# 128 zero products, 192 columns wide, in eight places of TensorE's order in chunks 1 to 3

## The chip, the core and the metric

The kernel runs on one core of one Trainium2 chip. A core has a matrix engine (TensorE, PE in the profile; its weight loads are a row of their own, PEld), three engines for element-wise work (VectorE = DVE, ScalarE = ACT, GpSimd = POOL) and a queue that mostly issues transfers (SyncE = SP). Each engine works through its own list of instructions in order; where one needs another's result it waits on a semaphore. The metric is the device time of one execution in microseconds (us). Before the change it is 824.97 us, the median of five runs: 825.07, 822.38, 826.83, 820.85 and 824.97.

## The reference

Two blocks, one after the other. The first is a recurrence over 768 steps for each of 4 batches and 8 heads, with a 40 x 40 state:

```python
for t in range(S):
    kt, vt, rt = (k[:, :, t], v[:, :, t], r[:, :, t])
    wt, at, bt = (w[:, :, t], a[:, :, t], b[:, :, t])
    y[:, :, t] = np.einsum('bhd,bhde->bhe', rt, state)
    Sa = np.einsum('bhde,bhe->bhd', state, at)
    state_decay = state * wt[:, :, None, :] - np.einsum('bhd,bhe->bhde', Sa, bt)
    state = state_decay + np.einsum('bhd,bhe->bhde', vt, kt)
```

Its result, turned to 3072 tokens of 320 values, goes through the second block, whose weights are 320 x 2048 and 2048 x 320:

```python
h = x @ w_in
g = h * np.cos(h)
return (g @ w_out).astype(np.float32)
```

## The kernel before

The sequence is cut into 24 chunks of 32 steps (`NCH`). A chunk of the recurrence has five steps in a row, `t, q, x, s, z` (functions `ch_t` to `ch_z`): the state is transposed (`sT`, line 558), multiplied with r (`qps`), combined with products prepared for the chunk (`x0ps`), multiplied with the chunk's inverted triangle (`sps`, which needs `rt`), and added up to the new state and the output (`dps`). Preparation of coming chunks is cut into steps too: `v, k, g` turn v, r and k and form the products `gram` for the next chunk; `pw, pa, pb, pn` turn w, a and b (`wT`, `aps`, `bT`) and form `nps` for later pairs of chunks. For four chunks at a time the triangles are inverted on VectorE alone (`inv_step`, lines 468 and 472), ending in `rt` (line 476).

The second block is cut into pieces over groups of 256 tokens (two chunks) and four slices of the 2048 hidden values: `first_a` and `first_b` make `ph` = x @ w_in in two tiles, ACT and DVE turn these into `gT` = h cos h (lines 730 to 740), and `second` multiplies them with w_out and adds up in `po`, one tile for each chunk of the group, over the four slices. A piece can only run when its chunks' outputs are there.

The weights come as words of a wider type and are rounded on the chip (`rounded`): DVE and ACT take them apart, DVE multiplies, POOL puts the sign on. These steps run until about 150 us.

The order on every engine is written out by hand in one Python loop over the chunks: for each chunk there is a list `segs` of steps, in which `M` marks a place where one piece of the second block goes (`piece`). `step` runs one entry and then lets queued-up work follow: steps of the inversion and of the weights (`fill` says how many of each) and work put off with `later` (transfers above all, which SP issues in that order). Since every engine works in order, an entry that waits on TensorE holds up all products behind it.

In chunks 0, 1 and the beginning of 2 there are already products of zeros on TensorE that nobody reads: `busy(n)` issues n of them, 512 columns wide, in bfloat16, from the tile `idle`, after each step. `shifted` puts 111 and 75 products of one column in two places. `mm` (line 101) issues all products but the transposes, so they all have that line in the profile.

On-chip accumulators (PSUM) are three pools of two tiles each: `ps_a` for the recurrence, `ps_h` for `ph` and the existing zero products, `ps_o` for `po` and, early on, `aps`. A `po` tile has 512 columns, of which the sums take 320 (`DM`).

## Time and profile before

| | us |
|---|---|
| median of five runs | 824.97 |
| lowest, highest | 820.85, 826.83 |
| the profiled execution | 825.07 |
| its span, first to last instruction | 823.1 |
| TensorE busy | 745.8 (91%) |
| VectorE busy | 508.1 (62%) |
| ScalarE busy | 384.0 (47%) |
| GpSimd busy | 200.7 (24%) |
| mean granted clock of TensorE | 0.95 of full |

The page gives busy time by engine over the span, and rows of 40 digits, one for each fortieth (20.6 us), in tenths; the row of the granted clock says how fast TensorE was allowed to run. The timeline lists instructions in order of time: start, busy time, engine, line, operation, output and inputs, shape and count, and in brackets how long the engine had been idle before and what ended that ("issue": nothing that the profile shows). Ends of products are modelled, so groups can overlap by a few tenths of a microsecond. A table of stretches gives for each the busy time of every engine, with the count of instructions, and the granted clock. The chain of waits follows the work back from the last instruction to what released it, step by step.

### The profile page before, as it was taken

How to read it: one execution, taken by the hardware profiler on the slowest of the kernel's cores; microseconds unless marked ns; L12 is line 12 of the kernel's file. 1: busy time of each engine (PE TensorE's matmuls, PEld its weight loads, DVE VectorE, ACT ScalarE, POOL GpSimd, SP SyncE). 2: the span in 40 equal slices, each digit the busy share in tenths (PEclk: the TensorE clock that was granted, in tenths of full speed). 3: DMA queues.
4: the chain of work that ended last, by engine and by line, in shares of the span. 5: the costliest groups of instructions: out<-in, count | busy, mean ns of one | idle time of the engine just before them, and what ended most of it. 6: DMA issues, size and time to landing. Idle time of an engine off the chain costs nothing.

```text
span 823.1 us, 37673 instructions
## 1 busy us (share of the span) xinstructions
PE 745.8 (91%) x16832; PEld 571.0 (69%) x16832; DVE 508.1 (62%) x1081; ACT 384.0 (47%) x707; POOL 200.7 (24%) x352
## 2 busy tenths in 40 slices
PE   3657678899689999999999999999999999999997
PEld 2534456677457777777777777777787777777775
DVE  6987888859645599354797553895444874332231
ACT  1214677544244553545446446435635445363352
POOL 5215554430214023212221230330230222201000
PEclk9856899899789999999999999999999999999999
DMA  7356663244043322333224324214210212101000
GB/s 124 76 131 164 175 165 103 47 120 71 22 100 85 62 58 52 70 99 68 52 39 74 65 61 69 60 37 69 61 41 24 46 35 52 21 21 37 20 17 16
DMA packets 183297, 55.66 MB, mean 68 GB/s; under 512 B 157152, under 2 KB 178656, under 8 KB 183136
## 3 DMA queue, kind: packets, MB, share of 16 engines
q1 hardware_dynamic: 180560, 51.95, 28.8%
q8 instruction: 132, 2.16, 1.1%
q10 hardware_dynamic: 2320, 0.98, 0.5%
q0 software_dynamic: 256, 0.33, 0.2%
q14 instruction: 29, 0.24, 0.1%
HBM read 42.07 MB, written 11.14 MB: 65 GB/s over the span
## 4 chain that ended last, share of the span: by engine, by line
PE 61%; DVE 20%; ACT 6%; DMA 5%; issue 3%; SPq 3%; POOL 1%; DVEq 0%; ACTq 0%; POOLq 0%
PE ph L101 21%; PE po L101 19%; DVE inv_tmp L468 4%; DVE inv L472 4%; PE dps L101 3%; PE x0ps L101 3%; SPq L152 3%; DVE rw L391 3%; PE gram L101 2%; PE vT L326 2%; PE sps L101 2%; PE qps L101 1%; DVE turns L732 1%; PE nps L101 1%; PE sT L558 1%
## 5 line engine op out<-in xcount | busy, mean ns | idle before, releaser
L101 PE MATMUL po<-w_out_sb,gT 128*128 128x320 f32 x768 | 227.0, 445 | 0.0
L101 PE MATMUL ph<-xT,w_in_sb 128*128 128x256 f32 x768 | 189.4, 392 | 4.4 <-DVE gT L740 3.7
L101 PEld LDWEIGHTS po<-w_out_sb,gT 128*128 128x128 f32 x768 | 142.5, 193 | 55.9 <-issue 4.2
L101 PEld LDWEIGHTS ph<-xT,w_in_sb 128*128 128x128 f32 x768 | 142.5, 194 | 33.5 <-issue 13.8
L730 ACT ACTIVATE turns<-ph,rnd 128x512 f32<-128x512 f32 x96 | 63.9, 686 | 157.2 <-PE ph L101 156.7
L732 DVE SCALAR_TENSOR_TENSOR turns<-turns,ph 128x512 f32<-128x512 f32 x96 | 63.7, 683 | 108.9 <-ACT turns L730 108.5
L740 DVE TENSOR_TENSOR gT<-ph,turns 128x512 f32<-128x512 f32 x96 | 65.6, 685 | 36.3 <-ACT turns L737 36.3
L657 POOL TENSOR_TENSOR qz<-qz,wc 128x160 f32<-128x160 f32 x92 | 43.4, 490 | 159.3 <-DVE qz L656 158.7
L472 DVE TENSOR_TENSOR inv<-inv,inv_tmp 128x31 f32<-128x31 f32 (+15 forms) x186 | 71.9, 386 | 6.4
L468 DVE TENSOR_TENSOR inv_tmp<-u,inv 128x31 f32<-128x31 f32 (+15 forms) x186 | 70.2, 377 | 4.4
L736 ACT ACTIVATE turns<-turns 128x512 f32<-128x512 f32 x96 | 60.2, 627 | 23.5 <-DVE turns L732 23.5
L737 ACT ACTIVATE turns<-turns,half_pi 128x512 f32<-128x512 f32 x96 | 69.3, 722 | 3.1
L490 POOL COPY vp<-nat_v 128x320 f32<-128x320 f32 x25 | 12.2, 488 | 183.2 <-DMA nat_v<-in_v_dram 166.6
L101 PE MATMUL ph<-xT,w_in_tail 64*128 64x256 f32 x384 | 54.6, 403 | 0.0
L656 DVE TENSOR_TENSOR qz<-dps,qz 128x160 f32<-128x160 f32 x92 | 28.9, 314 | 34.6 <-PE dps L101 34.5
L391 DVE RECIPROCAL rw<-nat_w 128x320 f32<-128x320 f32 x20 | 42.8, 2141 | 0.1
L562 ACT COPY s<-sT 128x512 f32<-128x512 f32 x46 | 24.5, 584 | 38.0 <-PE sT L558 38.0
L101 PEld LDWEIGHTS ph<-xT,w_in_tail 64*128 64x128 f32 x384 | 33.2, 187 | 10.3 <-issue 6.6
L668 POOL TENSOR_TENSOR yt<-yt,wb 128x512 f32<-128x512 f32 x24 | 31.4, 1309 | 22.4 <-DVE yt L663 22.4
L546 ACT COPY vvm<-gram 128x256 f32<-128x256 f32 x24 | 8.8, 368 | 54.8 <-DVE ag L541 54.4
L101 PE MATMUL sps<-x,rt 32*32 32x72 f32 x1536 | 22.7, 239 | 11.3 <-DVE rt L476 9.0
L101 PEld LDWEIGHTS sps<-x,rt 32*32 32x32 f32 x1536 | 18.0, 109 | 21.4 <-issue 16.6
(118 smaller groups left out, 1067.9 us busy)
## 6 DMA issues: line engine op xcount, KB each, us to landing
words<-in_moe_w_in_dram SPq DMA_DIRECT2D x8, 512.0 KB
nat_k<-in_k_dram SPq DMA_DIRECT2D x96, 40.0 KB
nat_v<-in_v_dram SPq DMA_DIRECT2D x96, 40.0 KB
nat_r<-in_r_dram SPq DMA_DIRECT2D x96, 40.0 KB
xd<-yt SPq DMA_DIRECT2D x48, 80.0 KB
out_dram<-ot SPq DMA_DIRECT2D x24, 160.0 KB
nat_b<-in_b_dram SPq DMA_DIRECT2D x88, 40.0 KB
wd<-ws SPq DMA_DIRECT2D x5, 640.0 KB
```

The costliest lines, as they stand in the source:

```text
L101: nc.tensor.matmul(o, lhsT=lhsT, rhs=rhs, start=start, stop=stop, skip_group_check=True)
L391: nc.vector.reciprocal(rw, wn)
L468: nc.vector.tensor_tensor(tmp, u[:, j : j + 1, :j].to_broadcast([P, C - j, j]), x[:, j:, j : j + 1].to_broadcast([P, C - j, j]), ALU.mult,)
L472: nc.vector.tensor_tensor(x[:, j:, :j], x[:, j:, :j], tmp, ALU.subtract)
L656: nc.vector.tensor_tensor(z, pick(dp, 0, (2 * N72 + C, 2), (N72, 2), (1, D)), z, ALU.add)
L657: nc.gpsimd.tensor_tensor(z, z, wc.rearrange("p (f m b) -> p f m b", f=2, m=2)[:, :, :, bb] .unsqueeze(3).to_broadcast([P, 2, 2, D]), ALU. ...
L668: nc.gpsimd.tensor_tensor(yt.rearrange("p j b t -> p (j b) t"), yt.rearrange("p j b t -> p (j b) t"), wx, ALU.mult)
L730: nc.scalar.activation(n, u, ACTF.Identity, bias=rnd, scale=1.0)
L732: nc.vector.scalar_tensor_tensor(n, n, -ROUND, u, ALU.add, ALU.subtract)
L736: nc.scalar.activation(n, n, ACTF.Abs)
L737: nc.scalar.activation(n, n, ACTF.Sin, bias=half_pi, scale=-2.0 * math.pi)
L740: nc.vector.tensor_tensor(gT[:, 2 * e : 2 * e + 2].rearrange("p f t -> p (f t)"), us[e], ns[e], ALU.mult)
```

## The change

`second` keeps the whole tile of 512 columns and slices it where it is used. A new helper `kept_busy(n)` issues n products of the zero tile `idle`, 128 x 128 weights by 192 columns in bfloat16, into the columns 320 to 511 of a `po` tile: of the tile of the running sum where there is one (then it adds zeros there), otherwise of a fresh tile of the same pool. A table `FILL` says where: key (chunk, place in `segs`), value the number of products, issued ahead of that entry. In chunk 1 that is ahead of `x` (12) and `z` (16); in chunk 2 ahead of `t` (10), `q` (14), `k` (6) and of the third `M`, which is `first_a` of the second piece (37); in chunk 3 ahead of `q` (13) and of `pa4`, the transposes `aps` of chunks 4 and 5 (20). Together 128. The existing `busy` calls stay.

```diff
     def second(g, j, i):
 
         if j == 0:
-            G["po", i] = ps_o.tile([P, 512], F32, tag="o", name="po")[:, :DM]
-        po = G["po", i]
+            G["po", i] = ps_o.tile([P, 512], F32, tag="o", name="po")
+        po = G["po", i][:, :DM]
...
+        def kept_busy(n):
+
+            if not n:
+                return
+            ps = G.get(("po", 0))
+            if fresh := ps is None:
+                ps = ps_o.tile([P, 512], F32, tag="o", name="spare")
+            for m in range(n):
+                mm(ps[:, DM:], idle, pick(idle, 0, (0, 2), (1, (512 - DM) // 2)), fresh and m == 0)
...
+        FILL = {(1, 4): 12, (1, 7): 16, (2, 0): 10, (2, 2): 14, (2, 3): 6, (2, 8): 37, (3, 3): 13, (3, 4): 20}
         for c in range(NCH):
...
             for i, seg in enumerate(segs):
+                kept_busy(FILL.get((c, i), 0))
                 while seg is s and ("rt", c) not in G:
```

## The prediction

> **What bounds the kernel now.** I read the page first, then TensorE's timeline, then busy time in stretches of 3.41 us.

> ```profile
> PE 745.8 (91%) x16832; PEld 571.0 (69%) x16832; DVE 508.1 (62%) x1081; ACT 384.0 (47%) x707; POOL 200.7 (24%) x352
> PEclk9856899899789999999999999999999999999999
> PE 61%; DVE 20%; ACT 6%; DMA 5%; issue 3%; SPq 3%; POOL 1%; DVEq 0%; ACTq 0%; POOLq 0%
> ```

> TensorE is busy for 91% of the span and makes 61% of the chain that ended last. One digit of the clock row is 20.6 us: after about 245 us it is full to the end, before that it dips. So the kernel is bound by TensorE from about 245 us on, and what the change can move is when that long stage begins. The eight places lie between 84 and 146 us. TensorE's timeline shows the wait in each (start, busy time, and in brackets the idle time before with what ended it):

> ```profile
> 85.60 0.88 PE L101 MATMUL x0ps<-vvm,ag 32*32 32x72 f32 x64 [1.61 <-ACT qz L574]
> 99.42 0.32 PE L101 MATMUL dps<-idle 32*64 32x288 bf16 x4 [2.50 <-DVE sm L622]
> 103.19 1.38 PE L558 MATMUL sT<-ident,qz 128*128 128x128 f32 x8
> 108.47 0.86 PE L101 MATMUL qps<-rT,s 40*40 40x32 f32 x64 [1.52 <-ACT s L562]
> 111.38 0.63 PE L326 MATMUL kT<-ident,kn 128*128 128x128 f32 x4 [0.87 <-issue]
> 124.17 3.35 PE L101 MATMUL ph<-xT,w_in_sb 128*128 128x256 f32 x8 [3.75 <-DVE gT L740]
> 127.45 0.88 PE L101 MATMUL sps<-x,rt 32*32 32x72 f32 x64
> 142.37 0.81 PE L101 MATMUL qps<-rT,s 40*40 40x32 f32 x64 [1.46 <-ACT s L562]
> 145.26 1.97 PE L326 MATMUL aps<-ident,nat_a 128*128 128x128 f32 x8 [2.08 <-ACT wb L374]
> 163.90 0.63 PE L326 MATMUL aps<-ident,nat_a 128*128 128x128 f32 x4 [2.21 <-DMA nat_a<-in_a_dram]
> 213.13 1.25 PE L101 MATMUL sps<-x,rt 32*32 32x72 f32 x64 [7.53 <-DVE rt L476]
> ```

> Seven of the eight places are real waits for another engine; the one at 103.19 is not. The granted clock changes only at steps of 3.41 us, so I cut the trace there (stretch, length, TensorE busy, weight loads, DVE, ACT, POOL, then granted clock and DMA):

> ```profile
> 65.57:68.98 3.41, 3.41 (x139) 2.33 (x137) 1.48 (x5) 3.08 (x5) 0.11 (x1) 0.50 0.39 59
> 120.18:123.59 3.41, 0.25 (x28) 0.13 (x16) 2.74 (x7) 3.35 (x7) 1.44 (x2) 1.00 0.88 282
> 123.59:127.01 3.42, 2.83 (x7) 2.33 (x8) 2.92 (x6) 2.46 (x4) 0.93 (x3) 0.50 0.38 108
> 140.66:144.07 3.41, 1.06 (x66) 0.70 (x64) 3.41 (x5) 3.41 (x7) 2.11 (x2) 1.00 0.73 216
> 161.14:164.55 3.41, 1.20 (x9) 0.99 (x10) 1.91 (x1) 0.65 (x2) 0.86 (x1) 1.00 0.38 62
> 212.34:215.75 3.41, 2.62 (x67) 2.06 (x68) 1.44 (x4) 0.49 (x2) 0.00 (x0) 0.50 0.00 0
> 215.75:219.17 3.42, 3.42 (x22) 1.74 (x29) 1.76 (x1) 0.00 (x0) 0.86 (x1) 0.50 0.00 0
> ```

> A stretch with little work (0.25, 1.06, 1.20 us) is followed by one at half clock; one at half clock is left after a full stretch (3.41, 3.42, and also 2.83), not after 2.62. (A stretch with 2.17 us, mostly small products, at 89.46 also fell to half.) Zeros count: the full stretch at 65.57 was partly the existing zero products.

> **The change part by part.** *The edit of `second`* slices the same tile in another place; TensorE issues the same products. Nothing.

> *Removed, moved:* nothing. Instruction order shows 128 weight loads and 128 products more on TensorE, none of them waiting, and no wait changed on any engine. Only what is behind them on TensorE can be delayed.

> *Price of one.* Zero products 512 columns wide took 1.03 us for four and 1.25 for five at full clock, so 0.22 us each, 0.43 ns per column, 0.082 us for 192 columns. Upper end: eight 128-column f32 transposes with a weight load each took 1.04 us and four 0.60, so 0.11 each. I take 0.085, nearer the row with the same data and the same load; 128 of them are 10.9 us (10.5 to 14.1).

> *Place by place, work against wait, in us:* 12 are 1.02 against 1.61; 16 are 1.36 against 2.50; 10 are 0.85 with no wait; 14 are 1.19 against 1.52; 6 are 0.51 against 0.87; 37 are 3.15 against 3.75; 13 are 1.11 against 1.46; 20 are 1.70 against 2.08. So 10.0 of 10.9 us lie in waits. The uncovered 0.85 delays the transposes sT, which end at 104.57 and are copied by ACT only at 107.36, so 2.8 us of slack hides them; without it they would cost 0.85. At 0.11 the 37 overrun by 0.32, the 20 by 0.12 and the 14 by 0.02.

> *Instruction supply.* The instruction queue shows 132 packets and 2.16 MB for 33,664 loads and products, so about 256 instructions a packet. TensorE's waits marked "issue" inside gram (0.92, at 88.4) and sps (1.28, at 91.8) sit 256 instructions apart, so a block that comes late costs up to 1.3 us. The 256 added instructions make one block more and leave the later cuts where they were; between the places the cuts move. Ahead of the 37 one cut falls in the last products of gram (ends 120.4). Bounds: 0, or 1.3 less the 0.6 spare, so 0.7. I take 0.3, the middle, because no row decides it. [...]

> *What the zeros buy.* The 37 lift the stretch at 120.18 from 0.25 to about 3.2 us busy, so the next is granted full clock. The eight ph there took 3.35; the same eight took 1.99 at 117.21. That is 1.36, less 0.3: 1.06. It is on the path: sps follows at once, ACT's copy of it ends 2.38 us of idle time on DVE (sm at 128.89), ACT itself having idled 1.16 before it, so up to 1.16 passes. I take 1.0. From there the chain of waits runs over ph, ACT's turns and DVE's queue to the reciprocal at 150.66, the loads that SP issues behind it, and the nat_a that lands at 163.90: about 1.0 early all the way.
> The 13 and 20 lift the stretch at 140.66 from 1.06 to about 3, so the ones at 144.07 and 147.49 run at full clock: 5.6 us of half-clock work, up to 2.8. I count none, because DVE's queue (aT, reciprocal, 147 to 153 without a gap but 0.85) sets what comes next; if that cover is thin it is up to 2.8 more. The first five places buy nothing I count: ACT and DVE, busy with the weight words, release what follows.

> *Given on.* At 163.90 ph runs at half clock from 164.55. Starting 1.0 earlier, 1.0 more of it lies ahead of 164.55 at full clock, which saves 0.5: 1.5. DVE's inverse carries that to rt, so sps starts at 211.6, not 213.13. The stretch from 212.34 is then full and the half clock ends at 215.75, not 219.17. Of 6.04 us at half clock (3.02 at full) 4.1 are left, doing 2.05; the other 0.97 runs at full clock to 216.7: 2.45. The half-clock stretches from 236.23 I leave as they are. Sum: 825.07 (the profiled execution: span 823.1 and 2.0 around it) less 2.5, so 822.6; the median 824.97 lies 0.1 below it: **822.5 us.**

> [...]

> **The rivals.**
> *A, as above* (0.40): 821 to 824.
> *B, the clock gain grows* (0.33): with the chain early, the stretch at 161.14 holds about 1.65 us of work (rows at full clock stayed there with 1.81 and 1.89, fell with 1.20), and the one at 232.82 may also hold enough. The first turns the rest of the half-clock ph, 1.2, into gain; the second 5.97 us of half-clock work, 3.0; a thin cover at 144 up to 2.8. So 2.5 plus 1.2 to 5.8: 816.5 to 821.4, likely 819. For it: after 92 us TensorE does 30 us of work at half clock, so 15 are lost. Against: nothing fills the 2.2, 7.5 and 2.4 us waits behind the last place.
> *C, hidden* (0.10): the 1.0 us is eaten in DVE's queue, where weight conversion is back to back from 131 to 147, or the steps fall so that no half clock followed the 3.75 us wait: 824 to 826.
> *D, the 37 overrun* (0.17), the other side. They start when gram's last products have their block. From a start later than 121.0 (124.17 less 3.15) ph is late; at 121.7 by 0.7. If by then the stretch holds only some 2.1 us, it may still fall to half clock: the 15 left at 123.59 take 2.6, ph starts at 126.2 and ends 2 us later than now. Then the later steps fall worse by one stretch (1.7) or two: 826 to 831.

> **How the numbers follow.** A measurement of this kernel can tell about 0.5% from no change: below 820.85 is faster, above 829.1 slower. Faster: 0.30 of B and 0.07 of A, 0.37. Slower: 0.13 of D. Same: the rest, 0.50. Range: a tenth below is B with most of its terms, 816.5; a tenth above is D at its worse end, 829.5. A's own range is 821 to 824.

> **What would show it.** Right: eight groups of 192-column products at 0.082 to 0.09 us pitch, idle of 0.3 to 1.1 us left behind them, clock 1.00 where 123.59 to 127.01 and 144 to 151 are now 0.50, sps of chunk 2 about 1 us earlier, rt's waiter near 211.6, no step down in the clock after about 245. Wrong: ph of the second piece later than 124.2; idle marked "issue" ahead of the zeros; sm at 128.89 unmoved; the half-clock stretches merely elsewhere; or TensorE no longer full in the long stage.

## The result and the profile after

The changed kernel takes 821.12 us (median of 35 runs, 817.18 to 823.21); the kernel before now 823.82 us (61 runs, 819.85 to 829.31). The ratio is 0.9966, 95% interval 0.9957 to 0.9976: 2.8 us faster (2.0 to 3.5), inside what was called "same" (0.5%). The prediction was 822.5 us, 2.5 less than a kernel before of 824.97; that kernel now measures 1.15 us less.

The page of the changed kernel, first engines, then the granted clock in slices of 20.5 us, then the instruction queue:

```profile
PE 747.4 (91%) x16960; PEld 575.3 (70%) x16960; DVE 509.5 (62%) x1081; ACT 384.0 (47%) x707; POOL 201.2 (25%) x352
PEclk9757999999789999999999999999999999999999
q8 instruction: 133, 2.18, 1.1%
```

128 products more, one packet of instructions more, and TensorE 1.6 us busier here, where the zeros alone are some 10.6: less of its other work runs at half clock (mean granted clock 0.962, before 0.950). How much less differs between executions: a second profile of each kernel (below) has 740.4 and 749.3 us, 8.9 apart. TensorE's timeline in five of the eight places, and at rt (a selection; start, busy time, idle time before and what ended it):

```profile
81.49 1.15 PE L101 MATMUL spare<-idle 128*128 128x192 bf16 x12
83.51 0.88 PE L101 MATMUL x0ps<-vvm,ag 32*32 32x72 f32 x64 [0.87 <-ACT qz L574]
91.54 1.48 PE L101 MATMUL spare<-idle 128*128 128x192 bf16 x16
97.32 0.32 PE L101 MATMUL dps<-idle 32*64 32x288 bf16 x4 [3.36 <-DVE sm L622]
105.23 1.32 PE L101 MATMUL spare<-idle 128*128 128x192 bf16 x14
106.47 0.81 PE L101 MATMUL qps<-rT,s 40*40 40x32 f32 x64
118.50 0.26 PE L101 MATMUL gram<-rT,vT 40*32 40x32 f32 x5 [0.24 <-issue]
118.69 3.23 PE L101 MATMUL spare<-idle 128*128 128x192 bf16 x37
122.09 1.97 PE L101 MATMUL ph<-xT,w_in_sb 128*128 128x256 f32 x8 [0.17 <-DVE gT L740]
123.98 0.88 PE L101 MATMUL sps<-x,rt 32*32 32x72 f32 x64
139.90 1.82 PE L101 MATMUL po<-idle 128*128 128x192 bf16 x20
141.79 1.09 PE L326 MATMUL aps<-ident,nat_a 128*128 128x128 f32 x8
207.91 1.25 PE L101 MATMUL sps<-x,rt 32*32 32x72 f32 x64 [7.53 <-DVE rt L476]
209.09 4.64 PE L101 MATMUL po<-w_out_sb,gT 128*128 128x320 f32 x8
```

The 37 products take 2.08 us more than the 12, so one takes 0.083 us. The wait for gT has shrunk from 3.75 to 0.17 us, and the eight ph behind the 37 take 1.97 us, not 3.35. Stretches of 3.41 us, cut at the steps of the clock of this execution (a selection; length, TensorE busy, weight loads, DVE, ACT, POOL, granted clock, DMA):

```profile
118.21:121.63 3.42, 3.18 (x48) 3.09 (x42) 2.74 (x7) 3.35 (x7) 1.58 (x3) 1.00 0.80 262
121.63:125.04 3.41, 3.24 (x78) 2.44 (x77) 2.80 (x6) 2.45 (x4) 0.90 (x2) 1.00 0.50 136
142.11:145.52 3.41, 3.41 (x24) 2.63 (x21) 2.56 (x5) 2.13 (x4) 2.45 (x3) 1.00 0.30 51
159.18:162.59 3.41, 2.28 (x12) 1.83 (x12) 1.91 (x4) 0.00 (x0) 0.86 (x1) 1.00 0.51 84
162.59:166.00 3.41, 3.41 (x142) 2.89 (x142) 2.13 (x2) 1.72 (x3) 0.86 (x1) 1.00 0.41 71
203.55:206.96 3.41, 0.00 (x0) 0.00 (x0) 3.05 (x8) 0.67 (x1) 0.00 (x0) 0.50 0.02 7
206.96:210.38 3.42, 2.47 (x67) 1.92 (x68) 1.45 (x4) 0.49 (x2) 0.00 (x0) 0.50 0.00 0
210.38:213.79 3.41, 3.41 (x15) 1.76 (x21) 1.91 (x1) 0.00 (x0) 0.86 (x1) 0.50 0.00 0
```

From 101 to 203 us the clock is full throughout; before there were half-clock stretches at 123.6, 144 and 164.5. The one after rt is as long as it was: 10.2 us.

The profiles end 4.6 us apart (spans 823.1 and 818.5), but 2.1 us of that is there at gT of the first piece (123.35 and 121.26), before the 37. In a second profile of each kernel taken later (runs b_again and a_again) gT comes at 122.73 and 122.33, 0.4 us apart, so I compare distances from there on. Worked out from the starts of the named instructions, in us:

| from - to | before | b_again | after | a_again |
|---|---|---|---|---|
| gT of the first piece - sm of chunk 2 (DVE) | 5.54 | 6.35 | 4.28 | 4.40 |
| sm - aT of chunks 4 and 5 (DVE) | 20.58 | 20.97 | 20.45 | 20.58 |
| that aT - aT of chunks 6 and 7 (DVE) | 15.20 | 14.26 | 15.08 | 14.15 |
| that aT - u, the inverse's beginning (DVE) | 15.84 | 14.22 | 14.21 | 14.22 |
| u - x0ps of chunk 5 (PE) | 62.88 | 61.06 | 62.78 | 62.99 |
| x0ps of chunk 5 - end | 579.6 | 580.6 | 580.4 | 581.8 |

The first row is the change's own gain, 1.1 to 2.1 us, in both pairs. The fourth is 1.6 us in one profile of before and nothing in the other: of the fourteen profiles of this case, the first of before is the only one with half clock there (at 164.5). Below that nothing is gained. From gT to the end it is 699.7 and 697.5 us before, 697.2 and 698.2 after, so two profiles of each do not show the 2.8 us; the 61 and 35 runs do.

### The profile page after: what moved, and what is told of

Read it like the earlier page. It is cut to its first block, busy times and chain, and to the rows that moved or that the text cites. A ratio compares the mean times of both kernels' runs of the same rounds, so it can differ in the third digit from the quotient of the medians.

```text
span 818.5 us, 37929 instructions
## 1 busy us (share of the span) xinstructions
PE 747.4 (91%) x16960; PEld 575.3 (70%) x16960; DVE 509.5 (62%) x1081; ACT 384.0 (47%) x707; POOL 201.2 (25%) x352
## 4 chain that ended last, share of the span: by engine, by line
PE 61%; DVE 20%; ACT 6%; DMA 4%; issue 3%; SPq 3%; POOL 2%; DVEq 0%; ACTq 0%; POOLq 0%
PE ph L101 20%; PE po L101 19%; DVE inv_tmp L468 4%; DVE inv L472 4%; PE dps L101 3%; PE x0ps L101 3%; SPq L152 3%; DVE rw L391 3%; PE gram L101 2%; PE vT L326 2%; PE sps L101 2%; PE nps L101 2%; DVE turns L732 2%; PE qps L101 1%; PE kT L326 1%
## 5 line engine op out<-in xcount | busy, mean ns | idle before, releaser
L101 PE MATMUL po<-w_out_sb,gT 128*128 128x320 f32 x768 | 226.9, 445 | 0.0
L101 PE MATMUL ph<-xT,w_in_sb 128*128 128x256 f32 x768 | 185.0, 385 | 0.7 <-DMA xT<-xd 0.5
L101 PEld LDWEIGHTS po<-w_out_sb,gT 128*128 128x128 f32 x768 | 142.5, 193 | 55.9 <-issue 4.2
L101 PEld LDWEIGHTS ph<-xT,w_in_sb 128*128 128x128 f32 x768 | 139.4, 190 | 29.1 <-issue 10.8
L740 DVE TENSOR_TENSOR gT<-ph,turns 128x512 f32<-128x512 f32 x96 | 65.6, 685 | 36.4 <-ACT turns L737 36.4
L101 PE MATMUL ph<-xT,w_in_tail 64*128 64x256 f32 x384 | 54.4, 402 | 0.0
L101 PEld LDWEIGHTS <-idle 32*64 32x64 bf16 (+2 forms) x566 | 24.4, 95 | 25.1 <-issue 19.0
L562 ACT COPY s<-sT 128x512 f32<-128x512 f32 x46 | 24.5, 584 | 36.5 <-PE sT L558 36.5
L101 PEld LDWEIGHTS ph<-xT,w_in_tail 64*128 64x128 f32 x384 | 33.0, 186 | 10.0 <-issue 6.3
L546 ACT COPY vvm<-gram 128x256 f32<-128x256 f32 x24 | 8.8, 368 | 55.8 <-DVE ag L541 55.4
L101 PEld LDWEIGHTS sps<-x,rt 32*32 32x32 f32 x1536 | 17.8, 107 | 21.3 <-issue 15.4
```

The costliest lines, as they stand in the source:

```text
L101: nc.tensor.matmul(o, lhsT=lhsT, rhs=rhs, start=start, stop=stop, skip_group_check=True)
L740: nc.vector.tensor_tensor(gT[:, 2 * e : 2 * e + 2].rearrange("p f t -> p (f t)"), us[e], ns[e], ALU.mult)
```

## The experiments

Most runs need products of one column instead of 192 that keep number and place. The helper got a switch for it:

```diff
-        def kept_busy(n):
+        def kept_busy(n, wide=True):
...
-                mm(ps[:, DM:], idle, pick(idle, 0, (0, 2), (1, (512 - DM) // 2)), fresh and m == 0)
+                if wide:
+                    mm(ps[:, DM:], idle, pick(idle, 0, (0, 2), (1, (512 - DM) // 2)), fresh and m == 0)
+                else:
+                    mm(ps[:1, DM : DM + 1], idle[:, :1], idle[:, :1], fresh and m == 0)
```

**All 128 one column wide (e1_narrow).**

```diff
-                kept_busy(FILL.get((c, i), 0))
+                kept_busy(FILL.get((c, i), 0), False)
```

> All 128 products stay in their eight places and in number, with their weight loads, but each is one column wide instead of 192, so every cut of the instruction blocks lies as in the changed kernel while TensorE stays nearly as idle as before. Theory (the clock: the gain comes from the busy time of the zeros): the gain is gone, ratio to before 0.999 to 1.002, and the stretch that holds the 3.75 us wait has under 1.5 us of TensorE work again and is followed by half clock. Rival (instruction supply: the gain comes from blocks fetched at other points): ratio 0.996 to 0.998, as with 192 columns. Rival (nothing local, only drift between executions): 0.999 to 1.002 and the same local distances as the changed kernel.

Measured: 0.9998 (0.9980 to 1.0016), 12 runs. The gain is gone, and the interval just clears that of the changed kernel (up to 0.9976). Its mean granted clock over the timed runs is 0.955, as before's (0.953); the changed kernel's is 0.962. In its profile (stretches and timeline):

```profile
120.42:123.83 3.41, 2.05 (x46) 1.86 (x47) 2.73 (x6) 2.98 (x6) 1.95 (x3) 1.00 0.32 123
123.83:127.24 3.41, 3.41 (x72) 2.30 (x70) 1.52 (x4) 1.69 (x3) 1.16 (x1) 0.50 0.50 154
120.70 0.26 PE L101 MATMUL gram<-rT,vT 40*32 40x32 f32 x5 [1.49 <-issue]
120.88 1.06 PE L101 MATMUL spare<-idle 128*1 128x1 bf16 x37
123.03 2.98 PE L101 MATMUL ph<-xT,w_in_sb 128*128 128x256 f32 x8 [1.08 <-DVE gT L740]
```

Same instructions in the same places, but ph is back to 2.98 us at half clock. The stretch has 2.05 us of TensorE work by these records, more than the 1.5 I wrote, and still the clock fell: the 1.06 us of one-column products did not hold it here. What the zeros give is the clock, not another supply of instructions.

**Only the 37 wide (e2_only37), all but the 37 (e3_narrow37), chunk 3's 33 alone (e4_chunk3), the first five groups alone (e10_first5).**

```diff
-                kept_busy(FILL.get((c, i), 0))
+                kept_busy(FILL.get((c, i), 0), (c, i) in ((2, 8),))
```

and with the other keys in the other runs.

> Only the 37 of chunk 2, ahead of the second piece's ph, are 192 wide; the other 91 are one column wide in their places. Theory (the 37 carry the gain, about 1.3 us there and what the clock adds later): ratio 0.9965 to 0.998. From the 37's ph to sps of chunk 2 takes 1.9 us, not up to 3.3. Rival (chunk 3's 33 carry it, through the half clock at 144 and later): 0.999 to 1.001. If each place gives a share: between.

> The counterpart: the 37 are one column wide, the other seven places 192 wide as in the changed kernel. Theory (the 37 carry the gain): ratio 0.999 to 1.000, ph ahead of sps of chunk 2 often at half clock. Rival (the first five or chunk 3's): 0.9965 to 0.998.

> Only the 13 and 20 of chunk 3 are 192 wide, the rest one column. My theory counted nothing for them, because VectorE's queue sets what follows: ratio 0.999 to 1.001, with full clock in the 7 us after them all the same. Rival (the cover on VectorE is thin): up to 2.8 us, ratio 0.9965 to 0.998. With the runs before, first five places alone = what is left of the changed kernel's gain.

> Of the 128 in their eight places only the first five groups (58) are 192 wide, the rest one column. I counted nothing for them: VectorE and ScalarE release what follows. Theory: ratio 0.999 to 1.001. Rival (they carry the part that the 37 and chunk 3's 33 do not, each measured at 0.999 alone): 0.9975 to 0.9985.

| run | wide | ratio | interval | mean clock |
|---|---|---|---|---|
| e2_only37 | 37 | 0.9988 | 0.9970 to 1.0005 | 0.957 |
| e3_narrow37 | 91 | 0.9992 | 0.9971 to 1.0013 | 0.958 |
| e4_chunk3 | 33 | 0.9993 | 0.9971 to 1.0014 | 0.957 |
| e10_first5 | 58 | 1.0011 | 0.9993 to 1.0029 | 0.955 |
| changed kernel | 128 | 0.9966 | 0.9957 to 0.9976 | 0.962 |

The first five buy nothing that can be measured. The shares of the 37 and of chunk 3 cannot be told apart by these times: each interval holds 1, and 0.0012 of the 37 is about half of what I expected. The three parts together (37, 33 and 58) add up to 0.0008, not 0.0034, but each is uncertain by some 0.002. The profiles are clearer: from gT of the first piece to sm of chunk 2 it takes 4.28 us with the 37 wide (e2) and 5.57 to 6.35 with them narrow (e1 5.57, e3 6.35, e4 5.61, e10 6.35), and ph in e2 takes 1.97 us:

```profile
121.86 0.25 PE L101 MATMUL gram<-rT,vT 40*32 40x32 f32 x5 [0.50 <-issue]
122.05 3.23 PE L101 MATMUL spare<-idle 128*128 128x192 bf16 x37
125.21 1.97 PE L101 MATMUL ph<-xT,w_in_sb 128*128 128x256 f32 x8
```

Chunk 3's zeros do what they should to the clock: ph after aps takes 1.89 us with them wide (e4, first line) and 3.04 with them narrow (e10, second line):

```profile
145.22 1.89 PE L101 MATMUL ph<-xT,w_in_sb 128*128 128x256 f32 x8
147.87 3.04 PE L101 MATMUL ph<-xT,w_in_sb 128*128 128x256 f32 x8
```

In the changed kernel's two profiles x0ps of chunk 3 then comes 0.44 us after aT of chunks 4 and 5, against 2.30 and 1.30 us in the two of before. But from that aT to the transposes of chunk 7, which wait for nat_a's transfer, it is 14.3 and 13.4 us after and 14.4 and 13.5 before. So nothing of it is handed on in these profiles.

**The kernels again, for a second profile (b_again, a_again).**

> The kernel before, unchanged, for a second profile. Theory (the steps of the clock fall anew in each execution): the half-clock stretches between 84 and 245 us begin at other points of the program, and the distance from gT of the first piece to x0ps of chunk 5, 120.0 us in the first profile, differs by 1 to 3 us. Rival (the steps are tied to the program's start): the same stretches and 120.0 within 0.3.

> The changed kernel, unchanged, for a second profile. Theory (steps of the clock fall anew in each execution, and the block ahead of the 37 comes at different times): gT of the first piece to x0ps of chunk 5 takes 115 to 119 us (116.8 in its first profile; 120.0 and 116.9 in the two of the kernel before); the wait for instructions ahead of the 37 lies between 0.2 and 1.5 us. Rival: both as in its first profile within 0.3 and 0.1.

One run each: 821.93 and 822.27 us. In the first profile of before the 45 steps of the clock from 65.57 to 219.17 us take 153.60 us, 3.413 each. Modulo 3.413 us the first recorded step lies 0.7, 3.1, 2.2 and 2.9 us from the start of the program (before, b_again, after, a_again): the steps fall anew in each execution. b_again has half clock at 122.5 to 129.3 (two stretches) and at 146.4, none at 164.5, and 6.8 us instead of 10.2 after rt. From gT to x0ps of chunk 5 before is 120.0 and 116.9 us, the changed kernel 116.8 and 116.3. The block ahead of the 37 came 0.24 and 0.87 us late; in the second case the zeros ended 0.3 us after gT was there:

```profile
120.19 0.26 PE L101 MATMUL gram<-rT,vT 40*32 40x32 f32 x5 [0.87 <-issue]
120.38 3.23 PE L101 MATMUL spare<-idle 128*128 128x192 bf16 x37
123.44 1.92 PE L101 MATMUL ph<-xT,w_in_sb 128*128 128x256 f32 x8
```

**64 instead of 37 (e6_over).**

```diff
-        FILL = {(1, 4): 12, (1, 7): 16, (2, 0): 10, (2, 2): 14, (2, 3): 6, (2, 8): 37, (3, 3): 13, (3, 4): 20}
+        FILL = {(1, 4): 12, (1, 7): 16, (2, 0): 10, (2, 2): 14, (2, 3): 6, (2, 8): 64, (3, 3): 13, (3, 4): 20}
...
+                if (c, seg) == (4, s):
+                    kept_busy(101, False)
```

> The 37 become 64 (5.5 us in a wait of 3.4 to 3.75), and 101 one-column products ahead of s in chunk 4, where TensorE waits 7.5 us, keep the later cuts of the instruction blocks in place (27 and 101 make 128). ph of the second piece then starts some 1.9 us late. Theory (this place is on the path to the end): 1.9 us slower than the changed kernel, ratio to before 0.998 to 1.000. Rival (VectorE's and ScalarE's queues set the end, and TensorE here has slack): 0.996 to 0.9975, unchanged.

Measured: 1.0020 (0.9999 to 1.0042): 4.4 us slower than the changed kernel by the ratios, 2.3 more than the overrun. In its profile ph comes 2.95 us after gT begins, not 0.83, and u is 55.75 us after gT, not 54.02 and 53.35: the overrun of 2.1 us arrives at the inverse nearly whole (1.7 and 2.4), so this place is on the path, as far as one profile shows it. The rest is a flaw of my experiment: between the 37 and the 101 there are 54 instructions more (27 loads and 27 products), so I reckon the cuts of the blocks 54 instructions off; a wait marked issue now stands between gram and sT:

```profile
180.93 0.73 PE L101 MATMUL gram<-rT,vT 40*32 40x32 f32 x62
184.38 1.86 PE L558 MATMUL sT<-ident,qz 128*128 128x128 f32 x8 [2.72 <-issue]
187.74 2.96 PE L101 MATMUL ph<-xT,w_in_sb 128*128 128x256 f32 x8
```

2.72 us of waiting marked issue, half clock behind it (183 to 190), and rt comes 34.6 us after u, not 30.6.

**Later cuts moved by half a block (e7_cuts).**

```diff
+                if (c, seg) == (4, s):
+                    kept_busy(64, False)
                 if seg is not M:
```

> The changed kernel and 64 one-column products ahead of s in chunk 4 (1.7 us in a 7.5 us wait): all later cuts of the instruction blocks move by 128 instructions, half a block. Theory (later waits for instructions are few and do not depend on the cuts): ratio 0.996 to 0.998 as the changed kernel. Rival (that 128 products make just one block is part of the gain): slower, 0.999 or more; by a late block of up to 1.3 us wherever small products come in a row.

Measured: 1.0101 (1.0069 to 1.0133), 11 us slower than the changed kernel for 64 one-column products in a wait of 7.5 us. My theory falls, the rival holds. What TensorE waited for after 250 us, in the changed kernel (the first three rows; total, times, longest):

```profile
PE vT L326 <- DVE vvm L547: 1.6, 3, 0.5
PE vT L326 <- ACT kT L521: 1.2, 3, 0.4
PE gram L101 <- issue: 1.0, 1, 1.0
```

and in this run (rows marked issue):

```profile
PE sps L101 <- issue: 2.0, 1, 2.0
PE dps L101 <- issue: 1.8, 4, 0.7
PE gram L101 <- issue: 1.5, 2, 1.2
PE nps L101 <- issue: 1.4, 2, 1.0
PE ph L101 <- issue: 1.1, 1, 1.1
```

The waits in this view add up to 12.4 us, against 5.9; those marked issue to 7.8 in ten places, against 1.2 in two. The clock, which in the changed kernel stays full there up to the last 0.6 us, falls too: half clock at 257 and 667 us behind waits marked issue (1.2 and 2.0 us), at 267 behind one of 1.4 us for POOL, 10.2 us together, some 5 lost. With the 6.5 us that is 11.6 of the 14.2 us by which the way from x0ps of chunk 5 to the end is longer in the profiles.

Cuts in the changed kernel's places do not rule such waits out. The profile of e4_chunk3, whose cuts lie as in the changed kernel, has 3.0 us of them in four places after 250 us, and one of 1.4 us was followed by half clock at 656; its way from x0ps of chunk 5 to the end is 584.6 us, not 580.4 and 581.8:

```profile
PE gram L101 <- issue: 2.6, 3, 1.4
652.96:656.38 3.42, 2.00 (x146) 1.67 (x135) 2.08 (x6) 0.61 (x3) 0.00 (x0) 1.00 0.02 5
656.38:659.80 3.42, 3.42 (x8) 2.13 (x7) 3.21 (x11) 0.16 (x1) 0.00 (x0) 0.50 0.00 0
```

**Three waits more filled (e5_more), that with a shorter 37 (e8_shorter), and the three alone (e9_late).**

```diff
+                more = {(3, 13): 20, (4, 12): 82, (5, 5): 26}.get((c, i), 0)
...
                 if seg is not M:
+                    kept_busy(more)
                     step(seg, *fill, small=seg in (q, x, g, s, z, pn, pn4))
```

e8_shorter also has 24 wide and 13 narrow in place of the 37; e9_late leaves out the call of the eight places.

> The changed kernel and 128 more products of the same kind in three waits that it left empty: 20 ahead of the transposes aps of chunks 6 and 7 (2.1 us wait inside them), 82 ahead of s in chunk 4 (7.5 us wait for rt), 26 ahead of nps in chunk 5 (2.4 us wait). Theory (the clock): the half clock after rt (10.2 us in both profiles, 6 us of work) and the one after the 2.4 us wait (6.8 us) go, 3 us and up to 3 us: ratio to before 0.990 to 0.994. Rival (these waits' followers are not on the path, or the zeros overrun): 0.996 to 0.999.

> The run with 256 products, but of the 37 ahead of the second piece's ph only 24 are 192 wide and 13 are one column wide, in the same place, so no cut moves. In two runs the last products of gram waited 1.1 and 1.5 us for their block, and the zeros then started at 120.9 to 121.1 and ran up to 2.2 us into ph's time. Theory (that overrun takes back part of the gain in some executions): 24 wide and 13 narrow take some 2.4 us instead of 3.2, ph is never later than its wait: 0.5 to 1 us better on average, ratio 0.988 to 0.991, with a smaller spread. Rival (the shorter filling lets the clock fall there again): 0.9915 to 0.994.

> Only the later three groups (20, 82 and 26), none of the change's eight places; again 128 products, one block. Theory (gains at separate half-clock stretches add up): 0.9915 less what the eight places give (0.9966), so 0.994 to 0.996. Rival (the eight places' lead is used up or doubled at the later half clock): 0.9975 to 0.999, or below 0.993.

| run | median us | ratio | interval | mean clock |
|---|---|---|---|---|
| e5_more | 817.23 | 0.9915 | 0.9886 to 0.9945 | 0.972 |
| e8_shorter | 820.34 | 0.9951 | 0.9931 to 0.9972 | 0.972 |
| e9_late | 821.51 | 0.9970 | 0.9952 to 0.9988 | 0.961 |

e5_more beats both kernels: 0.9886 to 0.9945 lies below the changed kernel's interval. Its timeline after the inverse:

```profile
203.80 6.93 PE L101 MATMUL po<-idle 128*128 128x192 bf16 x82
211.02 0.87 PE L101 MATMUL sps<-x,rt 32*32 32x72 f32 x64 [0.29 <-DVE rt L476]
211.82 2.42 PE L101 MATMUL po<-w_out_sb,gT 128*128 128x320 f32 x8
```

po takes 2.42 us, not 4.64 as in the changed kernel, because the clock stayed up over the 7.5 us wait. The 26 ahead of nps did less than expected: half clock of 3.4 us still follows there in e5_more (at 234.3) and e8_shorter (232.2), none in e9_late; it is 6.8 us in the changed kernel, but 3.4 in b_again too. The late three alone give 0.9970; with the eight places' 0.9966 the product is 0.9936, inside e5_more's interval, so gains at separate half-clock stretches add up as far as can be measured. In e5_more's profile rival D happened as well:

```profile
120.88 0.26 PE L101 MATMUL gram<-rT,vT 40*32 40x32 f32 x5 [1.14 <-issue]
121.07 4.88 PE L101 MATMUL spare<-idle 128*128 128x192 bf16 x37
125.79 1.92 PE L101 MATMUL ph<-xT,w_in_sb 128*128 128x256 f32 x8
```

The block came 1.14 us late, a half-clock step fell on the zeros, and ph began 3.08 us after gT, not 0.83. e8_shorter was to prevent that; in its profile it did (wait 0.50 us left before ph), but its time is not better than e5_more's, and the intervals overlap. Whether the shorter filling helps stays open.

**All fourteen profiles together.** Where half clock begins behind a wait, read from the granted clock of each profile:

| wait ahead of | zeros there wide | narrow or none |
|---|---|---|
| ph of the second piece (the 37) | 1 of 7 (e5_more, during the zeros) | 7 of 7 |
| aps of chunks 4 and 5 (the 20, and 13 before them) | 0 of 8 | 6 of 6 |
| s of chunk 4 (the 82) | 0 of 3 | 11 of 11 |

So in all of these cases but one the wide zeros hold the clock, though its steps fall elsewhere in each execution. What the 37 gain can be read at u: from gT of the first piece it takes 53.3 to 54.0 us in the five profiles in which they are wide (e8_shorter: 24 of them) and ph is at most 0.3 us late, 54.5 to 57.2 in the seven without, and 55.6 and 55.8 in the two in which ph is over 2 us late. The averages of the five and the seven are 53.6 and 55.7, about 2 us apart. Whether all of that reaches the end the profiles do not show: behind u two profiles of one kernel differ by 1 to 2 us, with 6.8 or 10.2 us of half clock after rt. Chunk 3's zeros make no such split: among the seven, the two that have them wide (e3, e4) take 55.6 and 54.5.

## Why the prediction was right, point by point

- *Price of one product*, 0.085 us (0.082 to 0.11): right, 0.083.
- *Only what is behind them on TensorE can be delayed, and ten in front of t cost nothing*: nothing contradicts it; the first five groups alone measure 1.0011 (0.9993 to 1.0029). That 0.3 to 1.1 us of idle time would be left behind each group came about right for x and k only. In the changed kernel's two profiles 3.36 and 1.42 us were left at z, and 0 to 0.34 ahead of q in chunks 2 and 3, of ph and of aps. The wait ahead of k, 0.87, was not one for another engine, as the prediction has it: its row says issue.
- *Instruction supply*, 0.3 us taken (0 to 0.7): the place was right, the late block is ahead of the 37 in every profile where they stand, but the bound was too tight: 0.24 to 1.14 us with them wide, up to 1.49 with them narrow. ph was late by 0 and 0.3 us in the changed kernel's two profiles, by 2.2 in e5_more's.
- *A late block costs up to 1.3 us*: too low, single waits marked issue took 2.0 us (e7_cuts) and 2.72 (e6_over). What they add up to depended on where the cuts fall: after 250 us 1.2 us in the changed kernel and 7.8 with the cuts half a block off, a run 11 us slower.
- *The cuts stay where they were, because 128 loads and products make one block*: right (133 packets), and worth far more than I had seen: see the half-block run.
- *What the 37 buy*, 1.06 at ph and 1.0 handed on: right in place and kind. ph takes 1.9 us instead of 3.4 to 3.8, sm of chunk 2 comes 1.1 to 2.1 us earlier, and an overrun there arrives almost whole at the inverse. At u it is about 2 us over all profiles, against 1.0 and the 0.5 given on before u. By time alone the 37 gave 0.0012 (-0.0005 to 0.0030).
- *Chunk 3's 33 count nothing, since VectorE's queue and the loads behind it set what follows*: right as far as the traces show; full clock and x0ps earlier, the transposes of chunk 7 not. Without the zeros, half clock followed the two waits there (1.46 and 2.08 us in the first profile) in both profiles of before, with 1.06 and 1.32 us of work in the stretch.
- *Given on*: both terms were off. The first counted 0.5 from a half clock at 164.5 that only the first profile of before has; in the changed kernel the stretch from 159.18 held 2.28 us, the next one had full clock, and aT to u took 1.6 us less than in that profile (rival B's first term, which the second profile of before had without any change). At rt I counted 0.95 from a shorter half clock; it was 10.2 us in both profiles of the changed kernel, against 10.2 and 6.8 before.
- *The sum*, 2.5 us: measured 2.8 (2.0 to 3.5). The range and the likeliest class held. That the number is so near is in part luck: the 37 brought about twice their 1.0, and the 1.45 given on did not come about as reckoned. One profile's steps of the clock were too little for such a sum: u to x0ps of chunk 5 differs by 1.8 us between the two profiles of before.
- *Rivals*: C (hidden) is excluded, since the interval ends at 0.9976. The time, 821.1, lies where A's range (from 821) and B's (to 821.4) overlap and does not decide between them; in the traces, of B only the first term came about, and not through the change. D was seen in e5_more's profile, in neither of the changed kernel's, and not in the median.

## What to carry to other kernels

In these runs zeros in a wait paid where the wait was followed at once by work on the path, and what they bought was the clock of the stretches behind it (without zeros at half clock for 3.4 and 6.8 us behind the wait for gT in the two profiles of before, for 10.2 behind rt in both of the changed kernel); judge each place by what the instruction behind it releases, not by how long it is idle. Count the instructions that are added: on an engine with 33,920 loads and products, where the blocks' cuts fall was worth 11 us (e7_cuts), four times the change itself. Where the clock's steps fall anew in each execution, compare distances between the same two instructions over several profiles, and the totals over many runs.

- 64 products of one column, which left 5.9 of the 7.5 us that TensorE waits for rt, made the run 11 us slower (e7_cuts, 1.0101 against 0.9966); with their loads they move the later instructions by 128, half a block (some 256, from 33,664 loads and products in 132 packets).
- TensorE work of 2.05 us in a stretch of 3.41, 1.06 of it one-column products, did not hold the clock (e1_narrow), nor did 2.00 us of mostly small products (e4_chunk3 at 652.96), while 2.28 us of full-width transposes and products did (the changed kernel at 159.18), and so did 1.81 and 1.89 us in before (at 82.63 and 106.53): the busy time of the records alone is not the measure.
- The 3.41 us steps started at another point of the program in each of four executions (0.7, 3.1, 2.2 and 2.9 us). After 250 us, where the first profiles of before and of the changed kernel have full clock up to their last 3.2 and 0.6 us, half clock followed waits of 1.2, 1.4 and 2.0 us (e7_cuts at 257, 267 and 667 us) and of 1.4 us (e4_chunk3 at 656); the one at 267 was for POOL, the others are marked issue.
